# Forming P-Q on VectorE from copies of P+Q and -2Q, with an accumulating transfer, in 67 of 200 pair steps

## The chip, the cores and the metric

The kernel runs on one core of a Trainium2 chip. A core has five engines that run side by side and meet at semaphores: TensorE (PE, matrix products into PSUM), VectorE (DVE), ScalarE (ACT), GpSimd (POOL) and SyncE (SP). Each executes its own instructions in order. SP and POOL also issue transfers (DMA), which run on their own and signal a semaphore when they have landed. The metric is the time of one execution on the device in microseconds (us); lower is better.

## The reference

```python
def _attn_ref(x):                      # x: 8 x 3008 x 256
    X = np.fft.fft(x, axis=1)
    X = np.fft.fft(X, axis=2)
    return X.real.astype(np.float32)

def _moe_ref(x, w_in, w_out):          # 24064 x 256, 256 x 2048, 2048 x 256
    h = np.maximum(x @ w_in, 0.0)
    return (h * h @ w_out).astype(np.float32)

def reference(**kwargs):
    ...
    attn_out = _attn_ref(**attn_kwargs)
    B, S, D = attn_out.shape
    x = attn_out.reshape(B * S, D)
    return _moe_ref(x=x, **moe_kwargs)
```

A two-dimensional Fourier transform of each of 8 sequences, of which the real part is kept, then two dense layers (FFN1 to 2048, FFN2 back to 256) with a squared ReLU between them.

## The kernel before

**The mathematics that the change touches.** The transform over the 256 features is folded into the first weight matrix: `gh` (128 partitions x 3 x 2048, f16) holds the cosine transform of `moe_w_in` in slot 0, the sine transform in slot 1 and, in slot 2, slot 1 times `turn2`. `zc` and `zs` hold the transform over the sequence, 128 feature rows by up to 512 columns each. For a column (a row k of the output) and its mirror (row S-k) the hidden layer before ReLU is P+Q and P-Q, with P = gh[0] zc and Q = gh[1] zs. Row 0 of `zs` and of gh[1] carries something else: the term of feature 128, which has the same sign in both. `turn2` is therefore -2 in every row but row 0, where it is 0: adding gh[2] zs to P+Q gives P-Q and leaves the term of feature 128 as it was.

**Windows and pair steps.** The 12,040 columns are cut into 25 windows (`wins`): six of 240 to 512 columns, 18 of 512 columns (windows 6 to 23) and a last one of 360. The loop `for w in range(NW)` runs over them. In each, eight pair steps (`NST = 8`) go over the 2048 hidden units, 2 x 128 at a time. A pair step of the kernel before is:

- `pq(s)`: four matmuls, P+Q for two groups of 128 hidden units, into a PSUM tile `ph` (2 x 512 f32; `ps_h` has two such buffers)
- `square(s, 0)`: ScalarE writes ReLU of `ph` as f16 into `h1` (three buffers, `h1p`), VectorE squares it into the first half of the window's `h2` (2048 x 1024, two buffers)
- `others(s)`: whatever else is spread over the steps: two jobs (16 matmuls) of FFN2 of the window before (`ffn2_steps`, with its copy to `osb` on ScalarE and its stores on SP), folds of the next batch of x on VectorE, its loads on POOL, matmuls and copies that make `zc` and `zs` of coming windows (`z_steps`; `minus` is its last VectorE piece)
- `turn(s)`: two more matmuls add gh[2] zs to the same `ph`, which turns P+Q into P-Q
- `square(s, 1)`: ReLU and square again, written in reverse order into the second half of `h2`

So a step has six matmuls of 512 columns for FFN1, two passes of ScalarE and two of VectorE.

**What sets the order.** The kernel writes its order out by hand: each engine executes its instructions in the order in which the program issues them. The first FFN2 job of a window reads the hidden units of steps 0 to 3 (chunks 0 to 7 of `h2`), the second those of steps 4 to 7; both stand in step 0 of the next window.

**Folds.** While window 5, 8, 10, 13, 16 or 19 is computed, a batch of x is folded (`fold_at`): `d_even` (VectorE: a copy, fe, a copy) in step 0, `n_cos` in step 1, `d_odd` (fo, and then the load of the next batch on POOL, with gathers) in step 2, `n_sin` in step 3, `odds` in step 4, `nyq` in step 5, `even` in step 6 (VectorE's ev, then POOL's transfer of it to DRAM, `scr`), `back` in step 7 (POOL: four transfers from `scr` to `rb`, which wait until `scr` has landed). Four later pieces (`late`: two of fold8, two of fold16) follow in steps 2 to 5 of windows 6, 9, 12, 15, 18 and 21.

**Memory that is used again.** `w16` holds the f16 copy of `moe_w_in` until `gh` is made. The tags `kf`, `tt` and `tm` of the pool `tmp` (two buffers each) hold the tables' intermediate results in the start and in window 2.

Of the kernel before, what the change touches and what calls it, by code (L numbers as in the profile page):

```python
# [8 lines left out]
F32 = mybir.dt.float32  # L9
F16 = mybir.dt.float16  # L10
I32 = mybir.dt.int32
AF = mybir.ActivationFunctionType
ALU = mybir.AluOpType

HS = 32.0
P = 128
# [3 lines left out]
def rev_dim(ap, i):  # L20

    dims = [list(d) for d in ap.ap]
    step, cnt = dims[i]
    dims[i] = [-step, cnt]
    return bass.AP(tensor=ap.tensor, offset=ap.offset + step * (cnt - 1), ap=dims)
# [3 lines left out]
def kernel(  # L29
# [14 lines left out]
    nc = tc.nc  # L44
    B, S, D = x.shape
    _, F = moe_w_in.shape
# [7 lines left out]
    NFC = F // P  # L54
    WN = 512

    FIRST = [240, 512, 376, 376, 512, 448]
    R23 = float(2.0 ** 23)

    RQ = (1, 3, 5, 0, 2, 4)  # L60

# [11 lines left out]
    wins = []  # L73
    g = 0
    while g < TOT:
        n = min(FIRST[len(wins)] if len(wins) < len(FIRST) else WN, TOT - g)
        wins.append((g, n))
        g += n
    NW = len(wins)

    def win_of(col):
        return max(w for w in range(NW) if wins[w][0] <= col) if col < TOT else NW
# [17 lines left out]
    const = ctx.enter_context(tc.tile_pool(name="const", bufs=1))  # L100
    tmp = ctx.enter_context(tc.tile_pool(name="tmp", bufs=2))
# [7 lines left out]
    drp = ctx.enter_context(tc.tile_pool(name="drp", bufs=2, space=bass.MemoryType.DRAM))  # L109
    ps_h = ctx.enter_context(tc.tile_pool(name="ps_h", bufs=2, space=bass.MemoryType.PSUM))  # L110
    ps_o = ctx.enter_context(tc.tile_pool(name="ps_o", bufs=2, space=bass.MemoryType.PSUM))
# [56 lines left out]
    perm = [const.tile([P, P], F16, name=f"perm{i}") for i in range(2)]  # L168
# [3 lines left out]
    nc.gpsimd.memset(idx["c"][0:2, :], P - 3)  # L172
    idx["f"] = iota([P, 1], [[1, 1]], -1, 1, "idx_f")
    nc.gpsimd.memset(idx["f"][0:1, :], 0)
    w16 = [const.tile([P, 2, F // 2], F16, name=f"w16_{i}") for i in range(2)]
    for i in range(2):
        nc.gpsimd.dma_start(out=w16[i], in_=moe_w_in[:, i * F // 2 : (i + 1) * F // 2].rearrange("(c p) f -> p c f", p=P))
    wout16 = const.tile([P, NFC, D], F16, name="wout16")
# [2 lines left out]
    def small(shape, name):  # L181
        return const.tile(shape, F32, name=name)
# [22 lines left out]
    def table_steps(e):  # L205
# [19 lines left out]
        def args(h):  # L225
            t = st["t", h] = tmp.tile([P, 3, NE], F32, name="t", tag="tt")
            for j in range(nr):
                r = row(h, j)
                if e == 0:
                    nc.scalar.activation(t[:, j, 0:n], st["kf"], AF.Copy, bias=R23, scale=vs[:, r : r + 1])  # L230
                else:
                    nc.vector.tensor_scalar(out=t[:, j, 0:n], in0=st["kf"], scalar1=vs[:, r : r + 1], scalar2=R23, op0=ALU.mult, op1=ALU.add)

        def turns(h):
            t = st["t", h]
            nc.vector.tensor_scalar(out=t[:, 0:nr, 0:n], in0=t[:, 0:nr, 0:n], scalar1=-R23, scalar2=-float(S), op0=ALU.add, op1=ALU.mult)

# [44 lines left out]
    at = const.tile([P, 2, P + 1], F32, name="at")  # L282
    for c in range(2):
        nc.scalar.activation(at[:, c, :], drow, AF.Copy, bias=R23, scale=dvs[:, c : c + 1])
    nc.vector.tensor_scalar(out=at, in0=at, scalar1=-R23, scalar2=-float(D), op0=ALU.add, op1=ALU.mult)
    for c in range(2):
# [141 lines left out]
    gh = const.tile([P, 3, F], F16, name="gh")  # L428
# [17 lines left out]
    def gh_turn(cc):  # L446
        f0 = cc * 512
        nc.vector.tensor_scalar(out=gh[:, 2, f0 : f0 + 512], in0=gh[:, 1, f0 : f0 + 512], scalar1=turn2[:, 0:1], scalar2=None, op0=ALU.mult)
# [3 lines left out]
    def zwin(w):  # L452
        if w not in zc:
            zc[w] = zp.tile([P, WN], F16, name="zc", tag="zc")
            zs[w] = zp.tile([P, WN], F16, name="zs", tag="zs")
        return zc[w], zs[w]
# [101 lines left out]
    for cc in range(1, F // 512):  # L558
        gh_turn(cc)

    def store(osb, p0, g0, m, minus, eng=nc.sync):

        for b, k0, kstep, n, c0 in runs:
            il, ih = max(g0, c0) - c0, min(g0 + m, c0 + n) - 1 - c0
            if minus and k0 in (0, H):
                il = max(il, 1)
            cnt = ih - il + 1
            if cnt <= 0:
                continue
            if minus:  # L570
                lo = p0 + (m - 1) - (c0 + ih - g0)
                row = b * S + S - (k0 + kstep * ih)
            else:
                lo = p0 + c0 + il - g0
                row = b * S + k0 + kstep * il
            eng.dma_start(
                out=bass.AP(tensor=out.tensor, offset=out.offset + row * D, ap=[[kstep * D, cnt], [1, D]]),
                in_=osb[lo : lo + cnt, :])
# [46 lines left out]
    def spread(jobs, i, n):  # L625
        return jobs[len(jobs) * i // n : len(jobs) * (i + 1) // n]
# [7 lines left out]
    fold_at, late_at = {}, {}  # L634
    for i in range(2, B):
        fold_at[win_of(col_of[i, 0]) - 2] = i
        late_at[win_of(col_of[i, 1]) - 2] = i
    NST = NFC // 2
    old = None
    for w in range(NW):  # L640
        g0, wn = wins[w]
        h2 = h2p.tile([P, NFC, 2 * WN], F16, name="h2", tag="h2")
        zcw, zsw = zwin(w)

        lo, hi = 0, NST - 1
        at = [[] for _ in range(NST)]
        post = [[] for _ in range(NST)]
        if w == 0:
            at[2] = [f0s["even"], f0s["back"]]
        elif w == 1:  # L650
            fj = fold_jobs(1)
            at = [[f] for f in fj[0:5]] + [[], [], []]
            post[5] = fj[5:6]
            lo, hi = 6, 7
        elif w == 2:
            te = table_steps(1)
            at = [[folds[1]["even"], lambda: te["freq"](), lambda: te["args"](0)], [lambda: te["turns"](0)], [lambda: te["mods"](0)],
                  [lambda: te["absm"](0)], [lambda: te["sins"](0)], [lambda: te["coss"](0)], [], [lambda: te["weigh"]()]]
            for st in range(4):
                at[st + 3] = at[st + 3] + f0s["late"][st : st + 1]  # L660
            at[7].append(folds[1]["back"])
        elif w in fold_at:
            fj = fold_jobs(fold_at[w])
            at = [[f] for f in fj[0:5]] + [[], fj[6:7], fj[7:8]]
            post[5] = fj[5:6]
        elif w == win_of(col_of[1, 1]) - 1:
            for st in range(4):
                at[st] = folds[1]["late"][st : st + 1]
            lo = 4
        if w in late_at:  # L670
            for st in range(4):
                at[st + 2] = at[st + 2] + folds[late_at[w]]["late"][st : st + 1]
        zj, zl = [], []
        for u in need[w + 1]:
            zu = z_steps(u)
            zj += [(zu, 0, 0), (zu, 1, 0), (zu, 0, 1), (zu, 1, 1)]
        f2 = ffn2_steps(*old) if old else []
        phs = {}

        def pq(s):  # L680
            ph = phs[s] = ps_h.tile([P, 2, 512], F32, name="ph", tag="psh")
            for a in range(2):
                f0 = (2 * s + a) * P
                nc.tensor.matmul(ph[:, a, 0:wn], gh[:, 0, f0 : f0 + P], zcw[:, 0:wn], start=True, stop=False)  # L684
                nc.tensor.matmul(ph[:, a, 0:wn], gh[:, 1, f0 : f0 + P], zsw[:, 0:wn], start=False, stop=True)  # L685

        def turn(s):
            for a in range(2):
                f0 = (2 * s + a) * P
                nc.tensor.matmul(phs[s][:, a, 0:wn], gh[:, 2, f0 : f0 + P], zsw[:, 0:wn], start=False, stop=True, skip_group_check=True)  # L690

        def square(s, sg):
            h1 = h1p.tile([P, 2, 512], F16, name="h1", tag="h1")
            nc.scalar.activation(h1[:, :, 0:wn], phs[s][:, :, 0:wn], AF.Relu)  # L694
            hv = rev_dim(h1[:, :, 0:wn], 2) if sg else h1[:, :, 0:wn]
            nc.vector.tensor_tensor(h2[:, 2 * s : 2 * s + 2, sg * wn : (sg + 1) * wn], hv, hv, op=ALU.mult)  # L696

        def others(s):
            for j in at[s]:
                j()  # L700
            for j in spread(f2, s, NST):
                j()
            for j in post[s]:
                j()
            if s == lo:
                zl[:] = [j for zu, part, h in zj for j in zu(part, h)]
            if s >= lo:
                for j in spread(zl, s - lo, hi - lo) if s < hi else []:
                    j()


        ng = 2 if w == 0 or wins[w - 1][1] < 384 < wn else 1
        for s0 in range(0, NST, ng):
            ss = range(s0, s0 + ng)
            for s in ss:
                pq(s)
            for s in ss:
                square(s, 0)
            others(s0)
            for s in ss:  # L720
                turn(s)
            for s in ss:
                square(s, 1)
            for s in ss[1:]:
                others(s)
        old = (w, h2)
    for j in ffn2_steps(*old, tail=True):
        j()
# [30 lines left out]
```

## Time and profile before

| what | value |
|---|---|
| runs of the kernel | 633.65, 633.65 and 635.58 us; median 633.65 us |
| span of the profiled execution | 632.0 us, 11586 instructions |
| TensorE, VectorE, ScalarE, GpSimd busy | 615.9, 369.5, 457.4, 76.5 us |
| FFN2 matmuls (L596) | 3024, 361.6 us busy |
| FFN1 matmuls (L684, L685, L690) | 400 each, 145.9, 145.9 and 112.8 us busy |
| ReLU on ScalarE (L694) | 400, 368.4 us busy |
| squares on VectorE (L696) | 400, 262.4 us busy |
| granted TensorE clock, mean | 1.000 |
| HBM read and written | 33.63 MB and 27.84 MB |

The profile is of one execution. Busy time is the time in which an engine had an instruction under way; matmuls overlap, so the sum of their durations says less than the distance from start to start. The chain is the work that ended last, followed back from the end: at each step to what released it, or to the instruction before it on its engine. A group's row has its line, engine, operation, output and inputs, shape and count, then busy time and mean duration in ns, then the idle time of the engine just before these instructions and what ended most of it. A DMA row has its queue, count, size and the median time from issue to landing.

### The profile page before, as it was taken

The page shows a single profiled execution, that of the slowest core. Times are in us where ns is not written, and L with a number is a line of the kernel's source. Part 1 is how long each engine was busy: PE and PEld are TensorE (multiplying, and loading weights), DVE is VectorE, ACT ScalarE, POOL GpSimd, SP SyncE. Part 2 cuts the span into 40 slices and gives each one's busy share as a digit, 9 for nine tenths or more (in the row PEclk, how much of TensorE's full clock was granted, in tenths as well). Part 3 has the DMA queues.
Part 4 walks back from the last instruction along what each step waited for, and adds up shares of the span by engine and source line. Part 5 has one row for each costly group of instructions (what it writes and reads, how often), then busy time and mean ns, then how long its engine had stood idle before and what let it go on. Part 6 is the DMA issues. An engine that isn't in the chain of part 4 may idle for free.

```text
span 632.0 us, 11586 instructions
## 1 busy us (share of the span) xinstructions
PE 615.9 (97%) x4548; PEld 439.1 (69%) x4548; DVE 369.5 (58%) x604; ACT 457.4 (72%) x610; POOL 76.5 (12%) x125
## 2 busy tenths in 40 slices
PE   5899999999999999999999999999999999999997
PEld 2457776776777767767777677777677776777786
DVE  7887656765457557645576455854557555454430
ACT  7787778777777677767777777777777777777662
POOL 5352200022002200220011100030000200000000
PEclk9999999999999999999999999999999999999999
DMA  8936211172112711631127211262111311111112
GB/s 146 211 82 127 85 34 34 50 164 78 36 43 58 184 46 42 144 97 35 51 44 160 74 52 39 59 151 73 40 31 55 111 34 47 38 46 35 49 54 65
DMA packets 36525, 47.52 MB, mean 75 GB/s; under 512 B 4216, under 2 KB 30328, under 8 KB 36472
## 3 DMA queue, kind: packets, MB, share of 16 engines
q0 software_dynamic: 9344, 22.14, 17.6%
q1 hardware_dynamic: 26899, 24.44, 12.7%
q8 instruction: 35, 0.57, 0.4%
q10 hardware_dynamic: 228, 0.21, 0.1%
q14 instruction: 19, 0.15, 0.1%
HBM read 33.63 MB, written 27.84 MB: 97 GB/s over the span
## 4 chain that ended last, share of the span: by engine, by line
PE 93%; DVE 3%; ACT 2%; issue 1%; POOL 0%; ACTq 0%; POOLq 0%; DVEq 0%
PE po L596 51%; PE ph L684 12%; PE ph L685 12%; PE ph L690 12%; PE pz L478 4%; ACT h L694 1%; PE pw L301 1%; DVE h L696 1%; PE pg L436 0%; ACT cos L259 0%; DVE fe L349 0%; DVE fo L353 0%; ACT sin L248 0%; ACT gh L440 0%; DVE od L368 0%
## 5 line engine op out<-in xcount | busy, mean ns | idle before, releaser
L694 ACT ACTIVATE h<-ph 128x1024 f16<-128x1024 f32 (+4 forms) x400 | 368.4, 974 | 80.0 <-PE ph L690 72.1
L696 DVE TENSOR_TENSOR h<-h 128x1024 f16<-128x1024 f16 (+4 forms) x400 | 262.4, 660 | 231.6 <-ACT h L694 228.2
L596 PE MATMUL po<-wout,h 128*128 128x256 f16 (+1 forms) x3024 | 361.6, 273 | 0.0
L596 PEld LDWEIGHTS <-h 128*128 128x128 f16 (+1 forms) x3024 | 296.8, 98 | 71.3
L684 PE MATMUL ph<-zc,gh 128*128 128x512 f16 (+4 forms) x400 | 145.9, 366 | 1.1 <-ACT h L694 0.8
L685 PE MATMUL ph<-zs,gh 128*128 128x512 f16 (+4 forms) x400 | 145.9, 366 | 0.4 <-ACT zs L487 0.4
L690 PE MATMUL ph<-zs,gh 128*128 128x512 f16 (+4 forms) x400 | 112.8, 366 | 2.0 <-ACT h L694 1.5
L611 ACT ACTIVATE osb<-po 128x512 f32<-128x512 f32 (+3 forms) x95 | 54.9, 582 | 57.4 <-PE po L596 52.4
L685 PEld LDWEIGHTS <-gh 128*128 128x128 f16 x400 | 39.1, 98 | 43.8 <-issue 2.5
L684 PEld LDWEIGHTS <-gh 128*128 128x128 f16 x400 | 39.0, 98 | 41.8 <-issue 0.5
L690 PEld LDWEIGHTS <-gh 128*128 128x128 f16 x400 | 37.2, 97 | 12.7 <-issue 4.3
L421 POOL COPY xt<-xt 128x2 f16<-128x2 f16 x16 | 2.5, 186 | 173.2 <-DVE xt L404 173.2
L130 POOL DMA_INDIRECT xo<-in_x_dram,idx_r x15 | 22.1, 1471 | 4.6 <-issue 4.6
L125 POOL DMA_DIRECT2D xo<-in_x_dram x8 | 6.0, 751 | 109.8 <-DVE fo L353 109.8
L483 ACT ACTIVATE es<-pz 128x376 f32<-128x376 f32 (+1 forms) x32 | 15.4, 481 | 5.3 <-PE pz L478 5.2
L391 POOL DMA_INDIRECT rb<-scr,idx_r x16 | 18.5, 1158 | 4.9 <-issue 4.9
L487 ACT ACTIVATE zs<-pz 128x376 f16<-128x376 f32 (+23 forms) x27 | 8.5, 358 | 9.9 <-PE pz L478 9.9
L349 DVE TENSOR_TENSOR fe<-xo 128x3072 f16<-128x3072 f16 x8 | 14.3, 1786 | 1.6 <-DMA xo<-in_x_dram,idx_r 1.3
L353 DVE TENSOR_TENSOR fo<-xo 128x3072 f16<-128x3072 f16 x8 | 14.2, 1779 | 0.0
L494 DVE SCALAR_TENSOR_TENSOR zc<-es,pz 128x376 f16<-128x376 f32 (+20 forms) x26 | 9.4, 392 | 7.2 <-ACT zc L487 7.0
L301 PE MATMUL pw<-spn 128*128 128x384 f16 x30 | 8.2, 448 | 5.2 <-DVE spn L290 5.2
L389 POOL DMA_DIRECT2D rb<-scr x16 | 8.8, 551 | 33.4 <-DMA scr<-ev 33.0
(106 smaller groups left out, 220.4 us busy)
## 6 DMA issues: line engine op xcount, KB each, us to landing
out_dram<-osb SPq DMA_DIRECT2D x77, 128.0 KB
xo<-in_x_dram POOLq DMA_DIRECT2D x7, 768.0 KB, 7.0
scr<-ev POOLq DMA_DIRECT2D x8, 390.0 KB, 4.4
rb<-scr POOLq DMA_DIRECT2D x16, 130.0 KB, 5.1
out_dram<-osb SPq DMA_DIRECT2D x12, 94.0 KB
w<-in_moe_w_in_dram POOLq DMA_DIRECT2D x2, 512.0 KB, 10.0
wout<-in_moe_w_out_dram POOLq DMA_DIRECT2D x1, 1024.0 KB, 14.5
out_dram<-osb SPq DMA_DIRECT2D x8, 75.0 KB
```

Of the source, the lines that this page charges most:

```text
L130: nc.gpsimd.indirect_dma_start(out=flat(q), out_offset=None, in_=bass.AP(tensor=x.tensor, offset=0, ap=[[XW, B * S * D // XW], [1, XW]]), ...
L301: nc.tensor.matmul(pw[:, 0 : 3 * P], spn[:, 0, 0, :], spn.rearrange("p c r d -> p (c r d)")[:, 0 : 3 * P], start=True, stop=True)
L391: nc.gpsimd.indirect_dma_start(out=rb[:, q].rearrange("p r d -> p (r d)"), out_offset=None, in_=bass.AP(tensor=src.tensor, offset=src.offs ...
L478: nc.tensor.matmul(ps[:, o0:o1], lhs, tab, start=(h == 0 and k == 0), stop=last, skip_group_check=True)
L483: nc.scalar.activation(es[:, 0:n], ps[:, 0:n], AF.Copy, bias=0.0, scale=1.0)
L596: nc.tensor.matmul(po[0:m, j * D : (j + 1) * D], h2[:, fc, q : q + m], wout16[:, fc, :], start=(fc == 0), stop=(fc == NFC - 1))
L611: nc.scalar.activation(osb[0:mm].rearrange("p s d -> p (s d)")[:, lo:hi], po[0:mm, lo:hi], AF.Copy, bias=0.0, scale=HS * HS)
L684: nc.tensor.matmul(ph[:, a, 0:wn], gh[:, 0, f0 : f0 + P], zcw[:, 0:wn], start=True, stop=False)
L685: nc.tensor.matmul(ph[:, a, 0:wn], gh[:, 1, f0 : f0 + P], zsw[:, 0:wn], start=False, stop=True)
L690: nc.tensor.matmul(phs[s][:, a, 0:wn], gh[:, 2, f0 : f0 + P], zsw[:, 0:wn], start=False, stop=True, skip_group_check=True)
L694: nc.scalar.activation(h1[:, :, 0:wn], phs[s][:, :, 0:wn], AF.Relu)
L696: nc.vector.tensor_tensor(h2[:, 2 * s : 2 * s + 2, sg * wn : (sg + 1) * wn], hv, hv, op=ALU.mult)
```

## The change

In windows 6 to 23 (`halved`), steps 0, 2, 3 and 5, or in windows that fold a batch steps 1, 3 and 5, the pair step takes another form: 67 of the 200 steps.

- `half_q(s)`: two matmuls write Q alone into `ph`. ScalarE copies it, times -2, as f16 into the first half of `sn`. VectorE writes into the second half of `sn` twice the term of feature 128, one instruction for each group of 128 hidden units: `eb` (row 0 of `zs`, the same in all partitions) times `wv` (twice row 0 of gh[1], one value for each hidden unit). A transfer issued by POOL adds the second half to the first.
- `others(s)` as before.
- `half_p(s)`: two matmuls add P to `ph`. ScalarE copies P+Q as f16 into the first half of `hd`. VectorE adds `sn` to it, reversed, into the second half (P-Q), takes the maximum with 0 over both halves, and squares both halves into `h2`.

`row_weights` makes `wv` once, in step 0 of window 3. `row_spread` makes `eb` for each window that has such steps: SP sends row 0 of `zs` to DRAM and then reads it back into all partitions. It is issued behind the last step of the window before. `sn` lies in the memory of `w16` (two buffers, used in turn), `eb` in `kf`, `hd` in `tt` and `tm` in turn.

```diff
+    MANY, FEW = (0, 2, 3, 5), (1, 3, 5)
...
-    w16 = [const.tile([P, 2, F // 2], F16, name=f"w16_{i}") for i in range(2)]
+    w16 = [const.tile([P, 2, F // 2], F16, name=f"w16_{i}", tag=f"w16_{i}") for i in range(2)]
...
+    wv = small([P, NFC], "wv")
+    def row_weights():
+        pv = ps_o.tile([P, 512], F32, name="pv", tag="po")
+        for fc in range(NFC):
+            nc.tensor.matmul(pv[:, fc : fc + 1], gh[:, 1, fc * P : (fc + 1) * P], perm[0][:, P - 1 : P], start=True, stop=True)
+        nc.vector.tensor_scalar(out=wv, in0=pv[:, 0:NFC], scalar1=2.0, scalar2=None, op0=ALU.mult)
+    eb = {}
+    def row_spread(w):
+        wn = wins[w][1]
+        zr = drp.tile([1, WN], F16, name="zr", tag="zr")
+        nc.sync.dma_start(out=zr[0:1, 0:wn], in_=zwin(w)[1][0:1, 0:wn])
+        t = eb[w] = tmp.tile([P, WN], F16, name="eb", tag="kf")
+        src = zr[0:1, 0:wn]
+        nc.sync.dma_start(out=t[:, 0:wn], in_=bass.AP(tensor=src.tensor, offset=src.offset, ap=[[0, P], [1, wn]]))
...
+    def halved(w):
+        if wins[w][1] < WN or w < 6:
+            return ()
+        return FEW if w in fold_at else MANY
+    ROT = [0]
...
+        if w == 3:
+            at[0].append(row_weights)
...
+        two = halved(w)
+        sns, hds = {}, {}
+        def half_q(s):
+            ph = phs[s] = ps_h.tile([P, 2, 512], F32, name="ph", tag="psh")
+            for a in range(2):
+                f0 = (2 * s + a) * P
+                nc.tensor.matmul(ph[:, a, 0:wn], gh[:, 1, f0 : f0 + P], zsw[:, 0:wn], start=True, stop=True)
+            i = ROT[0] % 2
+            sn = sns[s] = const.tile([P, 2, 2, WN], F16, name=f"sn{i}", tag=f"w16_{i}")
+            nc.scalar.activation(sn[:, 0, :, 0:wn], ph[:, :, 0:wn], AF.Copy, bias=0.0, scale=-2.0)
+            for a in range(2):
+                nc.vector.tensor_scalar(out=sn[:, 1, a, 0:wn], in0=eb[w][:, 0:wn], scalar1=wv[:, 2 * s + a : 2 * s + a + 1], scalar2=None, op0=ALU.mult)
+            nc.gpsimd.dma_start(out=sn[:, 0, :, 0:wn].rearrange("p a n -> p (a n)"), in_=sn[:, 1, :, 0:wn].rearrange("p a n -> p (a n)"), accum_op=ALU.add)
+        def half_p(s):
+            ph, sn = phs[s], sns[s]
+            for a in range(2):
+                f0 = (2 * s + a) * P
+                nc.tensor.matmul(ph[:, a, 0:wn], gh[:, 0, f0 : f0 + P], zcw[:, 0:wn], start=False, stop=True, skip_group_check=True)
+            hd = tmp.tile([P, 2, 2 * WN], F16, name="hd", tag=("tt", "tm")[ROT[0] % 2])
+            ROT[0] += 1
+            nc.scalar.activation(hd[:, :, 0:wn], ph[:, :, 0:wn], AF.Copy, bias=0.0, scale=1.0)
+            nc.vector.tensor_tensor(rev_dim(hd[:, :, wn : 2 * wn], 2), hd[:, :, 0:wn], sn[:, 0, :, 0:wn], op=ALU.add)
+            nc.vector.tensor_scalar(out=hd, in0=hd, scalar1=0.0, scalar2=None, op0=ALU.max)
+            nc.vector.tensor_tensor(h2[:, 2 * s : 2 * s + 2, :], hd, hd, op=ALU.mult)
...
+            if s0 in two:
+                half_q(s0)
+                others(s0)
+                half_p(s0)
+                continue
...
+        if w + 1 < NW and halved(w + 1):
+            row_spread(w + 1)
```

## The prediction

> **What bounds the kernel now.** I read the page's totals and chain first, then the groups by line, then single windows. On the page:
>
> ```profile
> PE 615.9 (97%) x4548; PEld 439.1 (69%) x4548; DVE 369.5 (58%) x604; ACT 457.4 (72%) x610; POOL 76.5 (12%) x125
> ...
> PE 93%; DVE 3%; ACT 2%; issue 1%; POOL 0%; ACTq 0%; POOLq 0%; DVEq 0%
> ...
> L696 DVE TENSOR_TENSOR h<-h 128x1024 f16<-128x1024 f16 (+4 forms) x400 | 262.4, 660 | 231.6 <-ACT h L694 228.2
> ...
> L690 PE MATMUL ph<-zs,gh 128*128 128x512 f16 (+4 forms) x400 | 112.8, 366 | 2.0 <-ACT h L694 1.5
> ```
>
> TensorE is busy throughout and carries 93% of the chain; L690 is the pass that the change drops. VectorE has 42% of the span free, nearly all of it waiting for ScalarE's h.
>
> The stretch view of windows 6 and 9 (both with late folds and work on z) and 23 (with neither), cut where TensorE starts each window's first L684; columns: us, then busy of PE, PEld, DVE, ACT, POOL, the granted clock, DMA share, GB/s.
>
> ```profile
> 140.08:165.01 24.93, 24.79 (x174) 16.83 (x173) 14.13 (x24) 19.15 (x25) 3.71 (x8) 1.00 0.24 70
> ...
> 214.90:241.14 26.24, 26.24 (x189) 18.38 (x188) 14.20 (x24) 19.02 (x25) 3.93 (x8) 1.00 0.21 62
> ...
> 571.18:595.51 24.33, 24.33 (x177) 17.22 (x176) 11.08 (x16) 17.46 (x21) 0.00 (x0) 1.00 0.14 44
> ```
>
> Windows 6 to 23, the only ones with new steps, run from 140.08 to 595.51: 455.4 us, 25.3 each. A plain window is 24.33 us of TensorE beside 11.08 of VectorE (16 squares of 0.692). So VectorE has room for 13 us per window, if it is never made to wait in between.
>
> **The change, part by part.** By the window rules 13 windows (6, 7, 9, 11, 12, 14, 15, 17, 18, 20 to 23) get four new steps (0, 2, 3, 5) and five (8, 10, 13, 16, 19, where a batch is folded) get three (1, 3, 5): 67.
>
> *TensorE.* Six matmuls of a step become four. Two 512-column matmuls less, starting 0.216 us apart (302.06, 302.28, 302.50, 302.71 in the timeline): 0.43 per step, 28.9 us in all. That is the whole gain.
>
> *ScalarE.* Two 128x1024 Copies for two Relus, 1.03 us either way: nothing. The 16 one-column matmuls and one small scaling of `row_weights` in window 3: under 1 us.
>
> *VectorE.* Two squares (1.38 us) go; a scaling per half (two of 128x512), the add, the max over 128x2048 and one square of 128x2048 come. The rows, by shape:
>
> ```profile
> L696 DVE TENSOR_TENSOR h<-h 128x1024 f16<-128x1024 f16 x320 | 220.4, 692 | 195.1 <-ACT h L694 195.0
> L349 DVE TENSOR_TENSOR fe<-xo 128x3072 f16<-128x3072 f16 x8 | 14.3, 1786 | 1.6 <-DMA xo<-in_x_dram,idx_r 1.3
> ...
> L368 DVE TENSOR_TENSOR od<-ab 128x1548 f16<-128x1548 f16 x7 | 6.8, 968 | 0.0
> ...
> L448 DVE TENSOR_SCALAR gh<-gh,turn 128x512 f16<-128x512 f16 x4 | 1.2, 349 | 0.0
> ...
> L265 DVE TENSOR_SCALAR cos<-cos,wge 128x377 f16<-128x377 f16 x2 | 0.5, 317 | 0.0
> ```
>
> Scalings: L448's form exactly, 2 x 0.349 = 0.70. Add: the 0.692 of a tensor_tensor of that size (reversed inputs cost the same there). Max: L265 to L448 gives 0.24 ns an element, so 0.349 + 1536 x 0.24 = 0.72. Square: from L368 to L349 it is 0.537 ns an element, 0.968 + 500 x 0.537 = 1.24. Together 3.35 us. Busy time alone would still fit under TensorE.
>
> *The wait.* VectorE works in order. In its new order the two scalings are followed directly by the add (in the folding windows and the late-fold steps by one fold of 0.42 to 0.97, which hides inside the wait). The add needs the accumulating transfer; the transfer needs the second scaling. So in every new step VectorE stands still for L = hand-over to POOL + issue to landing + hand-back, and behind the add queue max, square and the next steps' squares and scalings. Running ahead doesn't help: the scalings of the next new step stand behind the square of this one, so no two transfers overlap. Nor can TensorE leave VectorE behind: the second job of the FFN2 of a window runs in step 0 of the next and reads h of steps 4 to 7. Window after window the period is VectorE's own chain.
>
> No row shows an accumulating transfer, nor one inside SBUF. Nearest are the round trip of the even part, 390 KB out and 130 KB back (the last column is us to landing):
>
> ```profile
> scr<-ev POOLq DMA_DIRECT2D x8, 390.0 KB, 4.4
> rb<-scr POOLq DMA_DIRECT2D x16, 130.0 KB, 5.1
> ```
>
> and GpSimd's timeline around a quiet one and around a load of x:
>
> ```profile
> 212.86 0.60 POOL L381 DMA_DIRECT2D scr<-ev  x1 [7.37 <-DVE ev L379]
> 216.06 1.09 POOL L389 DMA_DIRECT2D rb<-scr  x2 [2.60 <-DMA scr<-ev]
> 217.46 1.23 POOL L391 DMA_INDIRECT rb<-scr,idx_r  x1 [0.30 <-issue]
> 218.99 0.98 POOL L391 DMA_INDIRECT rb<-scr,idx_r  x1 [0.30 <-issue]
> ...
> 252.68 0.75 POOL L125 DMA_DIRECT2D xo<-in_x_dram  x1 [17.63 <-DVE fo L353]
> 253.73 1.62 POOL L130 DMA_INDIRECT xo<-in_x_dram,idx_r  x1 [0.30 <-issue]
> 255.66 1.34 POOL L130 DMA_INDIRECT xo<-in_x_dram,idx_r  x1 [0.30 <-issue]
> ```
>
> The shortest landing of any of these direct transfers is 2.4 us, that of 390 KB is 2.8 at the least. The new one changes 256 KB and must read twice that. Lower end 2.4; upper end 5.2 (512 KB on the line through 390 KB in 4.4 and the 768 KB loads of x in 7.0). Most windows have a DMA share of 0.14 to 0.25, so I take 3.2, nearer the quiet rows. Hand-over: VectorE's ev ends at 212.56, POOL starts at 212.86, 0.3; hand-back 0.1, an estimate from the 0.1 between ScalarE's end and VectorE's start. L = 3.6 (2.8 to 5.6).
>
> The Trainium skill (DMA: Bandwidth & Descriptors, Anatomy of one DMA) fits a transfer issued by GpSimd as 2.0 us plus its bytes at 436 GB/s: 2.6 us for 256 KB. The quickest 390 KB row agrees (2.8 against 2.9), the median of 4.4 does not; with 2.6 the forecast would be 40 us lower.
>
> *Sum of VectorE's chain.* A window with four: 4 x (3.35 + L) + 8 squares 5.54 + about 1.0 of z and late fold outside the waits = 19.9 + 4L. A folding window: 3 x (3.35 + L) + 10 squares 6.92 + fe with its two copies 2.2, fo 1.78, od 0.97, ev 0.96, z 1.1 = 24.0 + 3L. All 18: 13 x 19.9 + 5 x 24.0 = 378.7, plus 67L = 241.2: 619.9 against 455.4, so +164.5.
>
> *Queues that the new transfers stand in.* (a) SP: `row_spread` sends one row to DRAM and back as a broadcast, one after the other, once the window's zs is complete. In windows 7, 12, 15, 18, 21 and 23 the last zs piece is made in step 6 of the window before, three squares (2.1 us) ahead of the first scaling; two small transfers of at least 2.4 and hand-overs make 5.6: 3.5 x 6 = 21. (b) POOL after a fold: scr, its landing and four rb issues (212.86 to 219.97, 7.1, with hand-over 7.4) stand ahead of step 0's transfer, whose scalings are done 2.8 after ev: about 4.6 x 5 = 23. (c) POOL with a load of x in step 2 of windows 8, 10, 13, 16: the issues take 4.6 from the end of fo and the gathers land in 8.7, so step 3's transfer, on the same queue, is in at about 12 instead of 5: +7, +7. In 13 and 16 POOL also waits for a gather (12.4 and 9.6 us from the first issue to the last): +11, +8. Together 33. Sum 77; 20 if most of it falls into other waits.
>
> 164.5 + 77 = +241 us. The profiled execution is a span of 632.0; the median of the runs is 633.65, 1.65 more for what lies around it. Forecast 633.65 + 241 = 875 us.
>
> **Rivals.**
> 1. *Faster*: the transfer hides and TensorE stays the bound, 633.65 - 28.9 = 604.8. It decides at 19.9 + 4L = 23.6, L = 0.9. For it: VectorE's and ScalarE's idle time. Against: no transfer in the trace lands in under 2.4.
> 2. *Quick transfers*: without DRAM on either side it lands in under 2.4 and (a) to (c) vanish in other waits. L = 2.2 and 20: 378.7 + 147.4 - 455.4 + 20 = +91, 725.
> 3. *Slow accumulation*: reading its destination costs more than the bytes say. With 6.0 to land, L = 6.4: +352 + 77, 1063.
> 4. *TensorE slows down when it idles.* The first 20 matmuls of 384 columns after an idle start took 6.29 us, 0.82 ns a column against 0.42 later. If the gaps kept it there, its 426.5 us in these windows become 853: +398, 1031. Against: it has some 24 us of work per 35, in long bursts. This is what the Trainium skill (TensorE: Matmul & The Clock Gate, What's actually happening) states: half clock after about 3.4 us idle, full again after as long busy; the start agrees, though the granted-clock column says 1.00 there. By it each gap costs some 1.7 us, inside VectorE's waits.
>
> **How the numbers follow.** Forecast 0.80, rival 2 0.07, rival 3 0.05, rival 4 0.03, rival 1 0.04, no change 0.01. The low end is landing 2.4 with 20 us of queues: 378.7 + 187.6 - 455.4 + 20 = +131, 765. The high end with L = 5.6 would be 1009; with POOL's waits partly shared I stop at 990. A measurement here can tell about 0.3% from no change. Slower 0.95, same 0.01, faster 0.04.
>
> **What would show it.** VectorE's add (L753) with a DMA as its releaser and 2.5 to 4 us idle ahead of most of the 67, TensorE's busy time down by 29 us but its share near 70%, waiting for VectorE in each window's step 0; the transfer's landing 2.8 to 4; windows of about 34 us; scalings 0.35, max 0.7, square 1.2. If adds wait mostly for ScalarE, or windows stay at 24 to 25 us, the theory is wrong.

## The result, and the profile after

The changed kernel takes 956.86 us (median of 4 runs, 950.73 to 958.16) against 633.74 us before (median of 4): the ratio is 1.507, 95% interval 1.503 to 1.512. That is 323 us more, where 241 were forecast, and inside the stated range of 765 to 990 us.

The page of the profile after: totals, the clock that TensorE was granted in 40 slices, and groups (busy time and mean ns; then the idle time just before them and its releasers). The last line is a DMA issue with its median time to landing.

```profile
span 956.0 us, 11734 instructions
...
PE 675.4 (71%) x4430; PEld 448.9 (47%) x4430; DVE 474.0 (50%) x806; ACT 462.4 (48%) x610; POOL 130.7 (14%) x192
...
PEclk8999998797888769887879788597878978686979
...
L753 DVE TENSOR_TENSOR hd<-hd,sn 128x1024 f16<-128x1024 f16 x67 | 46.4, 692 | 346.6 <-DMA sn<-sn 342.6
L728 DVE TENSOR_TENSOR h<-h 128x1024 f16<-128x1024 f16 (+4 forms) x266 | 164.3, 639 | 51.9 <-ACT h L726 48.6
...
L755 DVE TENSOR_TENSOR h<-hd 128x2048 f16<-128x2048 f16 x67 | 82.1, 1226 | 3.2
...
L742 DVE TENSOR_SCALAR sn<-eb,wv 128x512 f16<-128x512 f16 x134 | 40.9, 348 | 54.2 <-DMA eb<-zr 54.2
...
L754 DVE TENSOR_SCALAR hd<-hd 128x2048 f16<-128x2048 f16 x67 | 46.5, 693 | 2.3
...
sn<-sn POOLq DMA_DIRECT2D x67, 256.0 KB, 3.7
```

Two rows hold the loss. VectorE stood idle for 346.6 us in front of the 67 adds (L753), in 66 of the cases until an accumulating transfer had landed, and for 54.2 us in front of the scalings (L742), until eb had come back from DRAM. Together 401 us. That is more than the 323 us lost, because the idle time that VectorE had before, 231.6 us ahead of its squares, fell to 51.9 (L728), while its busy time rose by 104.5. No engine is busy throughout any more: TensorE has 71% of the span, VectorE 50%, ScalarE 48%. The durations of the new VectorE work are 0.348, 0.692, 0.693 and 1.226 us.

One window's quiet stretch on VectorE (window 12; start, duration, instruction, then in brackets the idle time ahead of it and what ended it):

```profile
412.14 0.61 DVE L742 TENSOR_SCALAR sn<-eb,wv 128x512 f16<-128x512 f16 x2
416.61 0.69 DVE L753 TENSOR_TENSOR hd<-hd,sn 128x1024 f16<-128x1024 f16 x1 [3.86 <-DMA sn<-sn]
417.34 0.69 DVE L754 TENSOR_SCALAR hd<-hd 128x2048 f16<-128x2048 f16 x1
418.14 1.22 DVE L755 TENSOR_TENSOR h<-hd 128x2048 f16<-128x2048 f16 x1
419.28 1.29 DVE L728 TENSOR_TENSOR h<-h 128x1024 f16<-128x1024 f16 x2
420.49 0.61 DVE L742 TENSOR_SCALAR sn<-eb,wv 128x512 f16<-128x512 f16 x2
```

From the end of the two scalings (412.75) to the add it is 3.86 us, and the next new step's scalings come only after this step's add, max and square and one normal step's two squares: a new step's transfer can't start while another is under way.

The longest of all waits, window 16, step 3. GpSimd first, then VectorE:

```profile
589.19 1.13 POOL L132 DMA_INDIRECT xo<-in_x_dram,idx_f  x1 [8.62 <-DVE fo L355]
597.04 0.54 POOL L143 DMA_DIRECT2D xo<-in_x_dram  x1 [6.72 <-DMA xo<-in_x_dram,idx_f]
...
600.71 1.02 POOL L743 DMA_DIRECT2D sn<-sn  x1
```

```profile
589.30 0.61 DVE L742 TENSOR_SCALAR sn<-eb,wv 128x512 f16<-128x512 f16 x2
589.83 0.96 DVE L363 TENSOR_TENSOR ab<-fo 128x1560 f16<-128x1560 f16 x1
609.97 0.69 DVE L753 TENSOR_TENSOR hd<-hd,sn 128x1024 f16<-128x1024 f16 x1 [19.18 <-DMA sn<-sn]
```

The scalings were done at 589.91, but POOL was held by the load of x until 600.71, and the transfer then landed 9.2 us later, while some 0.9 MB of the load's data moved on the same queue: 20.1 us from scaling to add.

### The profile page after: what moved, and what is told of

It is laid out like the page before. It is cut to its first block, busy times and chain, and to the rows that moved or that the text cites. A ratio compares the mean times of both kernels' runs of the same rounds, so it can differ in the third digit from the quotient of the medians.

```text
span 956.0 us, 11734 instructions
## 1 busy us (share of the span) xinstructions
PE 675.4 (71%) x4430; PEld 448.9 (47%) x4430; DVE 474.0 (50%) x806; ACT 462.4 (48%) x610; POOL 130.7 (14%) x192
## 5 line engine op out<-in xcount | busy, mean ns | idle before, releaser
L618 PE MATMUL po<-wout,h 128*128 128x256 f16 (+1 forms) x3024 | 402.1, 288 | 35.4 <-DVE h L755 24.6
L618 PEld LDWEIGHTS <-h 128*128 128x128 f16 (+1 forms) x3024 | 310.3, 104 | 143.2 <-DVE h L755 28.8
L726 ACT ACTIVATE h<-ph 128x1024 f16<-128x1024 f32 (+4 forms) x266 | 245.4, 949 | 241.4 <-DVE h L728 168.0
L753 DVE TENSOR_TENSOR hd<-hd,sn 128x1024 f16<-128x1024 f16 x67 | 46.4, 692 | 346.6 <-DMA sn<-sn 342.6
L728 DVE TENSOR_TENSOR h<-h 128x1024 f16<-128x1024 f16 (+4 forms) x266 | 164.3, 639 | 51.9 <-ACT h L726 48.6
L743 POOL DMA_DIRECT2D sn<-sn x67 | 58.3, 870 | 557.1 <-DVE sn L742 204.8
L722 PE MATMUL ph<-zs,gh 128*128 128x512 f16 (+4 forms) x266 | 79.9, 388 | 73.1 <-ACT h L726 72.8
L752 ACT ACTIVATE hd<-ph 128x1024 f16<-128x1024 f32 x67 | 68.7, 1026 | 120.3 <-PE ph L749 120.3
L717 PE MATMUL ph<-zs,gh 128*128 128x512 f16 (+4 forms) x266 | 107.6, 407 | 6.2 <-DVE zs L496 5.8
L740 ACT ACTIVATE sn<-ph 128x1024 f16<-128x1024 f32 x67 | 68.7, 1025 | 52.4 <-DVE hd L753 49.6
L755 DVE TENSOR_TENSOR h<-hd 128x2048 f16<-128x2048 f16 x67 | 82.1, 1226 | 3.2
L749 PE MATMUL ph<-zc,gh 128*128 128x512 f16 x134 | 47.8, 444 | 49.0 <-ACT sn L740 49.0
L742 DVE TENSOR_SCALAR sn<-eb,wv 128x512 f16<-128x512 f16 x134 | 40.9, 348 | 54.2 <-DMA eb<-zr 54.2
L722 PEld LDWEIGHTS <-gh 128*128 128x128 f16 x266 | 25.2, 99 | 83.5 <-issue 77.6
L375 PE MATMUL py<-od,perm 128*128 128x1 f16 x8 | 1.3, 166 | 87.2 <-DVE od L370 87.2
L754 DVE TENSOR_SCALAR hd<-hd 128x2048 f16<-128x2048 f16 x67 | 46.5, 693 | 2.3
L716 PEld LDWEIGHTS <-gh 128*128 128x128 f16 x266 | 28.5, 107 | 39.9 <-issue 19.9
L717 PEld LDWEIGHTS <-gh 128*128 128x128 f16 x266 | 28.6, 108 | 35.9 <-issue 16.4
L376 PEld LDWEIGHTS <-perm 128*128 128x128 f16 x8 | 0.8, 102 | 87.2 <-issue 87.0
```

The source lines that it names most:

```text
L618: nc.tensor.matmul(po[0:m, j * D : (j + 1) * D], h2[:, fc, q : q + m], wout16[:, fc, :], start=(fc == 0), stop=(fc == NFC - 1))
L740: nc.scalar.activation(sn[:, 0, :, 0:wn], ph[:, :, 0:wn], AF.Copy, bias=0.0, scale=-2.0)
L743: nc.gpsimd.dma_start(out=sn[:, 0, :, 0:wn].rearrange("p a n -> p (a n)"), in_=sn[:, 1, :, 0:wn].rearrange("p a n -> p (a n)"), accum_op=A ...
L752: nc.scalar.activation(hd[:, :, 0:wn], ph[:, :, 0:wn], AF.Copy, bias=0.0, scale=1.0)
L755: nc.vector.tensor_tensor(h2[:, 2 * s : 2 * s + 2, :], hd, hd, op=ALU.mult)
```

## The experiments

Eleven kernels were run. The first two take the wait for the accumulating transfer away, the next two hide or replace it, then come eb, the stores and the load of x, and at the end versions that keep what pays.

**A transfer that nobody waits for at the add.**

```diff
-            nc.gpsimd.dma_start(out=sn[:, 0, :, 0:wn]..., in_=sn[:, 1, :, 0:wn]..., accum_op=ALU.add)
+            nc.gpsimd.dma_start(out=aside, in_=sn[:, 1, :, 0:wn].rearrange("p a n -> p (a n)")[:, 0:944], accum_op=ALU.add)
```

> Edit: the accumulating transfer goes from the scaled half of sn into a tile that nothing reads (128x944 instead of 128x1024); so the term of feature 128 is not corrected in P-Q, and the add no longer waits for a transfer. Everything else of the changed kernel stays, the 67 transfers on POOL's queue among them. Theory (VectorE stands still at the add until the transfer has landed, 342.6 us in the changed kernel): those idle times go and about 605 to 670 us are left, the wait for eb (54 us) being what is still exposed. Rival (the transfers' traffic or POOL's work slows the other engines): 850 us or more. Second rival (VectorE's added busy time, some 105 us, is the bound): 720 us or more.

743.49 us. By the number alone this is the second rival's range (720 us or more), but VectorE's busy time is not the cause: nearly the same busy time (477 us here, 474 there) fits into a kernel of 617 us further down. The edit did not isolate what it was meant to. The add was free, but two other waits grew; from the list of waits of this run (engine and line, what it waited for, us in total, times, longest):

```profile
DVE sn L744 <- DMA eb<-zr: 123.3, 18, 17.8
...
ACT sn L742 <- DMA aside<-sn: 72.7, 14, 10.2
```

The transfer still reads the second half of `sn`, so ScalarE can't write the next -2Q into that buffer before it has landed. Ten of the 14 waits stand in step 3, for the transfer of step 0, whose scalings had themselves waited for eb. And VectorE, earlier than before, now ran into all 18 round trips of eb.

**No accumulating transfer at all** (the line above removed).

> Edit: the accumulating transfer is left out, so the term of feature 128 is not corrected in P-Q; both scalings on VectorE and the transfers that make eb stay. Theory: 605 to 670 us and within 10 us of the run whose transfers go into a tile that nothing reads. Rival (traffic): clearly below that run. Second rival (VectorE's busy time): 720 us or more.

668.15 us, inside the range of the theory, but 75 us below the run before, not within 10, and that was the sign given to the rival (traffic). The two waits shown above are large enough for it: ScalarE's 72.7 us are gone, and VectorE's wait for eb fell from 123.3 to 104.7. What traffic alone costs was not tried apart. So 289 us of the 323 go with the transfer, although in this run VectorE waits longer for eb than in the changed kernel: 104.7 us in front of 15 scalings, where it was 54.2.

**The add put off by one pair step.**

```diff
-        sns, hds = {}, {}
+        sns, late_v = {}, []
...
+            late_v.append((s, hd, sn))
+        def half_v():
+            s, hd, sn = late_v.pop(0)
             nc.vector.tensor_tensor(rev_dim(hd[:, :, wn : 2 * wn], 2), hd[:, :, 0:wn], sn[:, 0, :, 0:wn], op=ALU.add)
...
                 half_p(s0)
+                if len(late_v) > 1:
+                    half_v()
                 continue
...
+            while late_v:
+                half_v()
```

> Edit: nothing is left out and no instruction added; the add, the max and the square of a new pair step are put behind the VectorE work of the next pair step, so that the transfer has a step's time to land. Theory (the wait is exposed only because the add stands right behind the scalings): 620 to 720 us, the idle time ahead of the add under 100 us instead of 346. Rival (the transfers cannot be hidden, since the engine that is late is late by the sum of all waits): 850 us or more.

797.44 us (median of 4), ratio to the kernel before 1.258 (1.255 to 1.262). It is 159 us less than the changed kernel for nothing but another order of the same instructions, so where the add stands matters; but it missed the forecast of 620 to 720. The adds still waited 165.1 us instead of the under 100 expected, 13.5 us at the longest, and a new wait came, of TensorE's FFN2 for VectorE's squares:

```profile
DVE hd L757 <- DMA sn<-sn: 165.1, 42, 13.5
...
PE po L618 <- DVE h L759: 67.5, 18, 6.9
```

One pair step is too short a delay for 42 of the 67 adds. And the square of step 5, put off behind the two of step 6, is what the next window's second FFN2 job needs: each of the 18 waits stands at that job's first matmul on step 5.

**The correction on VectorE instead of a transfer.**

```diff
             for a in range(2):
-                nc.vector.tensor_scalar(out=sn[:, 1, a, 0:wn], in0=eb[w][:, 0:wn], scalar1=wv[...], scalar2=None, op0=ALU.mult)
-            nc.gpsimd.dma_start(out=sn[:, 0, ...], in_=sn[:, 1, ...], accum_op=ALU.add)
+                nc.vector.scalar_tensor_tensor(out=sn[:, 1, a, 0:wn], in0=eb[w][:, 0:wn], scalar=wv[...], in1=sn[:, 0, a, 0:wn], op0=ALU.mult, op1=ALU.add)
...
-            nc.vector.tensor_tensor(rev_dim(hd[:, :, wn : 2 * wn], 2), hd[:, :, 0:wn], sn[:, 0, :, 0:wn], op=ALU.add)
+            nc.vector.tensor_tensor(rev_dim(hd[:, :, wn : 2 * wn], 2), hd[:, :, 0:wn], sn[:, 1, :, 0:wn], op=ALU.add)
```

> Edit: nothing is left out; instead of two scalings and an accumulating transfer, VectorE forms wv x eb + (-2Q) in two scalar_tensor_tensor of 128x512 (estimate 0.65 to 0.75 us each, from the 0.607 of 128x376 f32), and the add reads that. No transfer is left but those of eb. Theory: 605 to 670 us; VectorE's chain is 4 x 4.0 + 6.5 = 22.6 us in a window with four such steps, under TensorE's 23.6. Rival (VectorE's busy time): 720 us or more.

703.99 us, ratio 1.110 (1.106 to 1.114): above the expected 605 to 670 and below the rival's 720. Two instructions of 0.746 us cost less than the 3.9 to 20 us from scaling to add, but the eb wait is there, 75.7 us in 12 cases:

```profile
L742 DVE SCALAR_TENSOR_TENSOR sn<-eb,wv,sn 128x512 f16<-128x512 f16 x134 | 94.4, 746 | 86.1 <-DMA eb<-zr 75.7 <-ACT sn L740 8.1 <-ACT h L726 2.3
```

**eb made once, with the transfers and without.**

```diff
-        t = eb[w] = tmp.tile([P, WN], F16, name="eb", tag="kf")
+        t = eb[w] = const.tile([P, WN], F16, name="eb1")
...
-        if w + 1 < NW and halved(w + 1):
+        if w + 1 == 6:
             row_spread(w + 1)
...
-                nc.vector.tensor_scalar(out=sn[:, 1, a, 0:wn], in0=eb[w][:, 0:wn], ...)
+                nc.vector.tensor_scalar(out=sn[:, 1, a, 0:wn], in0=eb[6][:, 0:wn], ...)
```

> Edit: the changed kernel with all its accumulating transfers, but eb is made once, for window 6, and used in all windows, so the term of feature 128 is right in window 6 alone; 17 of the 18 round trips over DRAM on SP's queue go. Theory (two waits in series on VectorE: eb 54 us, accumulating transfers 347 us): about 54 us less than the changed kernel, 895 to 915 us. Rival (the accumulating transfer's wait swallows it, since POOL's queue is busy behind a fold anyway): 935 to 957 us.

935.10 us: 22 less than the changed kernel, and here the rival was right. Of the 54.2 us at the scalings 5.6 were left, but the wait at the adds rose from 346.6 to 376.8. Nearly all of these 30 us stand in the first steps of the five windows after a fold: with eb at hand, VectorE finishes its scalings there before POOL is through with the fold's transfers, and POOL comes to the new transfer 5.1 to 8.1 us after them.

> Edit: no accumulating transfer (the term of feature 128 is not corrected in P-Q) and eb made once, for window 6. The scalings, copies, add, max and square of the 67 steps stay. Theory (with both waits gone TensorE is the bound again, VectorE's added busy time fits under it): 600 to 620 us, below the kernel before. Rival (VectorE's busy time bounds the folding windows): 630 us or more.

616.79 us, as the theory had it, 17 us below the kernel before. The page, and windows 15, 17 and 16 of the stretch view (us, then busy of PE, PEld, DVE, ACT, POOL, clock, DMA share, GB/s):

```profile
PE 589.5 (96%) x4430; PEld 426.3 (69%) x4430; DVE 474.2 (77%) x806; ACT 457.6 (74%) x610; POOL 80.0 (13%) x125
```

```profile
365.50:388.30 22.80, 22.80 (x169) 16.26 (x167) 19.19 (x33) 17.51 (x21) 1.23 (x4) 1.00 0.15 44
413.80:438.30 24.50, 24.50 (x182) 17.60 (x181) 18.79 (x33) 19.08 (x27) 4.03 (x5) 1.00 0.46 122
388.30:413.80 25.50, 24.42 (x196) 18.02 (x195) 23.75 (x37) 19.21 (x27) 5.25 (x6) 1.00 0.33 69
```

With both waits gone TensorE is full again, and VectorE's 474 us, the same busy time as in the 957 us kernel, fit beneath it. Window 15 takes 22.80 us, where the same window took 24.3 before. The folding window 16 gains nothing (25.5 us, 25.6 before): VectorE is busy for 23.75 of it and TensorE waits 1.1. The other four folding windows gain nothing either (24.7 to 25.6 us, 24.4 to 25.6 before).

**No stores in windows 6 to 23.**

```diff
     def store(osb, p0, g0, m, minus, eng=nc.sync):
+        if wins[6][0] <= g0 < wins[NW - 1][0]:
+            return
```

> Edit: the changed kernel without the stores of windows 6 to 23 (their rows of the output are not written). Theory (the accumulating transfer lands in 3.3 us when nothing else moves and in 5 to 8 us beside stores): nearly every landing at 3.2 to 3.4 us outside the loads of x, 40 to 70 us less than the changed kernel, 885 to 920 us. Rival (the long landings come from VectorE's or POOL's own state): landings as before, 945 to 957 us.

874.19 us, 83 less, more than the 40 to 70 expected. The wait at the adds fell from 346.6 to 311.0 us, that at the scalings from 54.2 to 9.8, so over half of the gain is at eb, which the theory had not named; the adds that waited over 4.2 us from 28 to 16. Of these 16, four stand behind the loads of x, and five are the first steps of the windows after a fold; the other seven were not followed up. One of the five, GpSimd and then VectorE:

```profile
263.72 0.58 POOL L383 DMA_DIRECT2D scr<-ev  x1 [6.98 <-DVE ev L381]
266.73 1.09 POOL L391 DMA_DIRECT2D rb<-scr  x2 [2.44 <-DMA scr<-ev]
268.13 1.02 POOL L393 DMA_INDIRECT rb<-scr,idx_r  x1 [0.30 <-issue]
269.46 0.99 POOL L393 DMA_INDIRECT rb<-scr,idx_r  x1 [0.30 <-issue]
270.45 1.01 POOL L746 DMA_DIRECT2D sn<-sn  x1
```

```profile
265.44 0.61 DVE L745 TENSOR_SCALAR sn<-eb,wv 128x512 f16<-128x512 f16 x2
273.98 0.69 DVE L756 TENSOR_TENSOR hd<-hd,sn 128x1024 f16<-128x1024 f16 x1 [7.93 <-DMA sn<-sn]
```

The scalings are done at 266.05, POOL comes to the transfer at 270.45, 4.4 us late. In the changed kernel this is hidden: there the scalings of the same windows came 6 to 9.6 us late for want of eb.

**eb by TensorE.**

```diff
-        nc.sync.dma_start(out=zr[0:1, 0:wn], in_=zwin(w)[1][0:1, 0:wn])
...
+        pe = ps_z.tile([P, 512], F32, name="pe", tag="pz")
+        nc.tensor.matmul(pe[:, 0:wn], sel, zwin(w)[1][:, 0:wn], start=True, stop=True)
         t = eb[w] = tmp.tile([P, WN], F16, name="eb", tag="kf")
+        nc.scalar.activation(t[:, 0:wn], pe[:, 0:wn], AF.Copy, bias=0.0, scale=1.0)
```

`sel` is a 128x128 matrix whose row 0 is one and whose other rows are zero, so that each output partition gets row 0 of `zs`.

> Edit: nothing is left out; the sum wv x eb - 2Q is formed by scalar_tensor_tensor as in the run without an accumulating transfer, and eb is made by one TensorE matmul for each window with a matrix whose row 0 is one, and a ScalarE copy, instead of the round trip over DRAM on SP's queue. Theory (the eb wait, 75.7 us there, goes; VectorE's 0.7 us instructions make the folding windows VectorE's): 620 to 645 us. Rival (the idle time comes back as waits for VectorE): 680 to 705 us.

633.73 us (median of 10), ratio 0.999 (0.997 to 1.002): the eb wait is gone, 70 us of it, and the time is that of the kernel before. By windows (from the last square of one to that of the next) the folding ones took 26.6 to 28.6 us against 24.4 to 25.6 before, the others 23.2 to 25.2 against 24.3 to 26.2.

**The load of x behind step 3's transfer.**

```diff
         def d_odd():
             nc.vector.tensor_tensor(fof[:, :, 1:129], lo, hi, op=ALU.subtract)
+        def load():
             if i + 1 < B:
                 xs[i + 1] = load_x(i + 1)
...
             post[5] = fj[5:6]
+            at[4] = fj[8:9] + at[4]
```

> Edit: nothing is left out; the changed kernel with the load of the next batch of x issued in step 4 instead of step 2 of a folding window, so behind step 3's accumulating transfer on POOL's queue instead of ahead of it. Theory (in windows 8, 10, 13 and 16 step 3's transfer stands behind the load; the adds there waited 11.65, 15.46, 15.63 and 19.18 us against 3 to 4 elsewhere): these four waits fall to about 4 each, part comes back in step 5, 905 to 935 us. Rival (the load delays the transfers by its traffic, wherever it is issued): 945 to 960 us.

922.21 us, 35 less, inside the expected range. The four adds waited 3.97, 3.91, 3.04 and 5.91 us, 45 us less together. But much of it came back, most in step 5, as in window 13, where POOL waits for a gather within the load: 10.80 us against 3.86. Over all 67 adds the wait fell only from 346.6 to 336.0 us. The larger part of the 35 us, 22 of them, is at the scalings (54.2 to 31.7), where the theory had not looked.

**A version that beats both.**

```diff
-    MANY, FEW = (0, 2, 3, 5), (1, 3, 5)
+    MANY, LATE, FEW = (0, 2, 3, 5), (0, 2, 3, 5), ()
```

on top of scalar_tensor_tensor and eb by TensorE:

> Edit: nothing is left out; the kernel with scalar_tensor_tensor and eb by TensorE, but with no new pair steps in the five folding windows (52 instead of 67 steps). There its folding windows took 26.6 to 28.6 us against 24.4 to 25.6 before the change, all others 23.2 to 25.2 against 24.3 to 26.2. Theory (VectorE's busy time bounds the folding windows alone): 618 to 626 us, faster than before. Rival (the loss moves into the next windows): 630 to 636 us.

620.92 us, ratio 0.980 (0.978 to 0.981).

```profile
PE 598.4 (97%) x4473; PEld 430.3 (70%) x4473; DVE 493.5 (80%) x761; ACT 464.3 (75%) x623; POOL 82.6 (13%) x127
```

Counted in the same way, the folding windows are back at 24.4 to 25.3 us, and TensorE has 97% of a shorter span.

> Edit: nothing is left out; as the run with no new steps in the folding windows, with the new steps at 0, 2, 4, 6 and, in windows with late folds, at 0, 3, 6 (46 steps). Theory (two new steps in a row, 2 and 3, let VectorE fall behind, and late folds add 2.2 us to its window): each window without late folds gains up to 0.4 us more, each with them loses 0.43 of TensorE's gain; 616 to 626 us. Rival (a new step at 6 delays the second FFN2 job of the next window): slower than the run with 52 steps by over 2 us.

622.30 us, ratio 0.981 (0.980 to 0.983): inside the expected range, 1.4 us behind the run with 52 steps. Neither the theory's gain from spreading nor the rival's loss of over 2 us shows; each of the six steps that it has less is 0.43 us of TensorE, 2.6 in all.

## Why the prediction was right, and where its sizes were off

**TensorE's gain of 28.9 us**: it exists. With the waits away, the kernel without transfers and with one eb was 17 us faster than before, 1.5 us in a plain window of the 1.7 that four steps should give. Most of the rest is missing in the folding windows, where VectorE is the bound, and some in window 6, which still waits 5.8 us for the one eb. The sum for a folding window (24.0 us of VectorE) had it a little under TensorE's time.

**VectorE's busy time alone would fit**: right outside the folding windows, as that same run shows. The durations were within 0.03 us of the forecast (0.348, 0.692, 0.693, 1.226).

**The wait L at the add**: the mechanism was right, its size was the term that failed. L was set at 3.6 us from quiet rows, because most windows have a low DMA share. When nothing else moves it is 3.9: POOL's issue 0.53 after the scalings, 3.24 to 3.35 us to land, 0.1 to the add. The sum took 3.6 for all 67. But the 63 adds outside the loads of x came 4.8 us after their scalings on average, and 24 of them over 4.5. That is 303 us where 227 were summed: 76 us of the 82 that the forecast was short. Some 20 of the 76 are the quiet value itself, 3.9 for 3.6. For the rest, what had not been counted is what the output's stores do to a transfer that is under way beside them; the range's upper end for L (5.6) came from larger transfers, not from this. In the run without stores the 58 adds outside the loads and outside the first steps after a fold came 4.1 us after their scalings on average, where the same 58 came 4.9 us after them here: 44 us. For L and for eb together that run was 83 us shorter.

The Trainium skill (DMA: Bandwidth & Descriptors, Anatomy of one DMA) gives a transfer 2.0 us plus its bytes at 436 GB/s, 2.6 for 256 KB; an estimate with the 512 KB that are read gives 3.2. The 3.24 to 3.35 of the undisturbed transfers agree with the second reading; beside stores the measurement decides, and no fit of size alone holds.

**(a) and (b), eb and the transfers after a fold**: 21 and 23 us were summed, 44 together; measured is 54.2, all of it at the scalings. That the two totals are near each other is in part luck, since the places were other ones. Of the six windows of (a) only 7 and 23 waited (2.2 and 4.9 us). Windows 9, 11, 14, 17 and 20, which follow a fold and where POOL was expected to be late, waited 39.9 us for eb, and the wait for POOL disappeared in it. It came to light in the run with eb made once, and, at the 4.2 to 4.4 us that had been worked out as 4.6, in the run without stores. The SP timeline before window 9 (row to DRAM, and broadcast back), first in the changed kernel and then in the run without stores:

```profile
273.63 0.38 SPq L578 DMA_DIRECT2D zr<-zs  x1
279.52 0.35 SPq L581 DMA_DIRECT2D eb<-zr  x1
```

```profile
222.92 0.22 SPq L578 DMA_DIRECT2D zr<-zs  x1
224.01 0.34 SPq L581 DMA_DIRECT2D eb<-zr  x1
```

In the changed kernel the last piece of this window's zs was written at 231.0, but the row left only at 273.63, since `row_spread` stands on SP's queue behind the stores of window 8. The prediction let it leave "once the window's zs is complete". It then took 5.9 us from the first to the second, where 2.4 and a hand-over had been assumed; VectorE's scaling followed at 283.10, after 8.79 us of waiting. Without the stores the row left with its zs, 42 us ahead of the scalings, took 1.1 us, and none of the five windows waited for eb. How much is the place behind the stores, and how much the slower trip beside the stores and the even part's transfer, was not tried apart.

**(c) the load of x**: four adds came 12.5, 16.3, 16.5 and 20.1 us after their scalings, 65 in all against 4 x 3.6 + 33 = 47. The place was right, as the run with the load behind the transfer shows.

**The chain without waits** was summed as 378.7 us for windows 6 to 23 and measured as 351: 773.5 from the end of window 5's squares to that of window 23's, less 368 from scaling to add and 54 at the scalings. VectorE's independent instructions overlap by some 0.08 us (the two scalings take 0.61 together, not 0.70), which no term had: the durations of its instructions in these windows add up to 395.5 us, but it was busy for 364.2. Beside the two waits it was idle for only 8.5 us there.

So +76, +10 and +18 for the waits and -28 for the chain make +76 of the 82 us; the remaining few lie outside these windows. That the chain was summed too long by 28 us, and so hid a quarter of what the waits were short, was luck.

**The signs that were named**: the adds' releaser is the transfer, as said. The idle time ahead of them, named as 2.5 to 4 us in most cases, had too low an upper end: 31 of 67 lie in it, and 28 lie over 4.2. Windows of about 34 us were forecast and 37 to 51 measured. TensorE's waits for VectorE were named for step 0 of each window; ahead of FFN2 (L618) the page has 35.4 us, but 87.2 us stand ahead of a small matmul of the folds (L375), which waits for `od`. TensorE's share is 71%, near the 70% named, but its busy time went up by 60 us instead of down by 29. That is rival 4's mechanism, without its price:

```profile
263.34 0.16 PE L375 MATMUL py<-od,perm 128*128 128x1 f16 x1 [14.35 <-DVE od L370]
...
264.20 0.63 PE L716 MATMUL ph<-zc,gh 128*128 128x512 f16 x1
264.63 0.63 PE L717 MATMUL ph<-zs,gh 128*128 128x512 f16 x1
...
269.05 0.38 PE L716 MATMUL ph<-zc,gh 128*128 128x512 f16 x1
269.27 0.38 PE L717 MATMUL ph<-zs,gh 128*128 128x512 f16 x1
```

After 14 us of waiting for a fold's VectorE work, 512-column matmuls start 0.43 us apart, and 0.22 apart some 5 us after the restart. The granted clock was 0.835 over the span and is 0.995 in the run with both waits gone. The Trainium skill (TensorE: Matmul & The Clock Gate, What's actually happening) states this as half clock after an idle window and full clock after a busy one; the two distances agree. What TensorE's slower pace cost by itself was not tried apart. The two waits account for the loss without it: VectorE was busy or in one of them for all but 8.5 of the 773.5 us of windows 6 to 23.

Of the other rivals, *faster* and *quick transfers* fell, since no accumulating transfer landed in under 3.24 us, where they needed under 2.4. *Slow accumulation* fell too: alone, the transfer lands in 3.24 to 3.35 us, near the 3.2 of the forecast and far from 6.0. That a transfer is slowed by the stores beside it stood in no rival, and that was the missing one.

## What to carry to other kernels

Idle time of an engine is room for work only if the work's inputs are there when it is its turn: an in-order engine that issues the first half of a chain, hands it to a transfer and takes it back in its next instruction waits the whole latency each time, here 3.9 us or more, 67 times, and the 42% of the span that VectorE had free were no help. Two vector instructions of 0.75 us were cheaper here than a transfer of 4 us and more, and one matmul of 512 columns with a ScalarE copy cheaper than a round trip of a row over DRAM. Price a transfer not by its quiet landing but with what shares its queue and its engines in that stretch, and when a wait is removed, look for the one that stood behind it.

## What the runs showed of the hardware that had not been expected

An accumulating transfer of 256 KB inside SBUF landed 3.24 to 3.35 us after its issue when next to nothing else moved, and in up to 7.5 us beside stores, outside the loads of x. A store of one row of 1 KB to DRAM and the wait for it, from its issue on SP to that of the load behind it, took 1.1 us where the queue was quiet (windows 7 and 10), 3.1 us before window 13 (441.32 to 444.41), and 3.0 to 7.4 us in the five windows after a fold, beside a 390 KB transfer and stores. A transfer that only reads a buffer holds up the engine that wants to write it next as surely as one that writes it: 72.7 us of ScalarE's waits in the run whose transfers nobody was to wait for.
